# A banded-attention and expert-layer kernel: second-part loads behind a fence, wider filler matmuls, one more preparation step per piece early on, ten pieces per attention step

## The chip, the core and the metric

The kernel runs on one core of one Trainium2 chip. Its metric is the device time of one execution in microseconds (us). The core has a matrix engine (PE in the profile, with its weight loads as PEld), a vector engine (DVE), a scalar engine (ACT), a general engine (POOL) and an engine that here only issues transfers (SP). Each runs its own instructions in program order and waits on semaphores for the others.

## What is computed

```python
scores = scale * np.matmul(q, k.transpose(0, 1, 3, 2))      # 4 batches, 8 heads, 576 rows, 64 wide
scores = np.where(masks[None, :, :, :], scores, -1000000000.0)
scores = scores - np.max(scores, axis=-1, keepdims=True)
attn = np.exp(scores)
attn = attn / (np.sum(attn, axis=-1, keepdims=True) + 1e-09)
x = np.matmul(attn, v)                                      # as 2304 rows of 512
p = domain_probs / (domain_probs.sum(-1, keepdims=True) + 1e-09)
for e in range(4):
    out += p[:, e:e + 1] * (np.maximum(x @ w1[e], 0.0) @ w2[e])
```

Four heads see the last 32 positions, four see every fourth of the last 128. With the rows of the latter reordered, every head has a band 32 wide.

## The kernel before

**Attention.** The work of the band is cut into 24 steps (0 to 23), each of two groups of 192 rows. A step passes through stages that lie on different engines: `s_qk` (PE, tile sc), `s_max` (DVE: mask, maximum), `s_sub` (POOL), `s_exp` (ACT), `s_sum` (DVE: sum and reciprocal rc), `s_norm` (POOL), `s_tr` (PE transposes pt, copied by ACT to pts), `s_av` (PE, tile po, copied by ACT into the raw activations xr). The main loop runs over `n`; in each round several steps are at different stages. Steps 0 to 4 are the first part, 5 to 9 the second, 10 to 23 the third; between parts three rounds pass without a new step.

**Expert layer.** The weights come in 16 units of 256 hidden columns (`u`). A visit `(u, m)` treats one unit and one of three blocks of 768 rows. The first product (`product`, L411, tiles m1x and m1y) is done in seven block products instead of eight, on sums of the operands; the second (`mm2`, L514, tile m) adds into acc on DVE (L522). Every operand is split into a high part (ACT, L129: xh, g1h, g2h, w2h) and a low part (POOL or DVE, L126: xl, g1l, g2l, w2l). The sums of activation blocks (`x_sums`, L223) run on DVE, those of weights (`w1_sums`) on POOL. `experts` is a generator; each `yield` is a piece, about six matmuls. The first two visits are plain (no sums), 14 pieces in each of two halves; each later visit has 13 pieces: five in `mm1_b`, two in the next visit's `mm1_a`, three and three in `mm2`.

**Order.** Everything is in a fixed program order. Rounds before `START` (7) hold attention and fillers (`dummies`, L743: matmuls of the identity, 256 columns, results unused), six a round. From `START` two pieces a round are taken; after the first half `experts` pauses until round `OPEN` (15) and fillers stand in. From `OPEN` on a round takes `PACE` pieces if it begins a step, else four. After each piece `step()` does one unit of `queue`: a list of preparations (weight splits, weight sums, activation splits and sums); `later` holds those that are less urgent. When the rounds are over (gate "over"), the next visit's `begin()` closes the attention's buffers, opens more PSUM banks (gate "m1"), and puts six activation splits and two `x_sums` of the last row block into `later`. They must be done (`need(x_sums, 5)`) when visit (14, 0) hands over to (15, 0). While the buffers of the attention are in use, tile m has two PSUM banks, afterwards four.

**Loads.** SP issues nearly all transfers, in the order of the list `loads`, as `ready` allows: `load_qk` (q 192 KB, k 224 KB a step), `load_v` (two of 192 KB), `fetch_w1` and `fetch_w2` (512 KB each), probs (36 KB), masks (192 KB, from ACT's queue).

Of the kernel before, what the change touches and what calls it, by code (L numbers as in the profile page):

```python
# [18 lines left out]
GB = 6  # L19
GS = GB // 2  # L20
GW = GB * QB
PACE = 11
GAP = 3
QKB = 3
VB = 4
FILL = 6


def band_masks(S):
# [20 lines left out]
def kernel(  # L50
# [11 lines left out]
    nc = tc.nc  # L62
# [177 lines left out]
    def attention(ap, xrp, pa):  # L240
# [22 lines left out]
                ap=[row, (two.offset - one.offset, 2), col],  # L263
            )

        def load_qk(gs, k_queue):
            q_s = ap.tile([128, 2, GW], F32, tag="q", name="q_s", bufs=QKB)
            k_s = ap.tile([128, 2, GW + WINDOW], F32, tag="k", name="k_s", bufs=QKB)
            nc.sync.dma_start(out=q_s, in_=both(qT, gs, GW))
            k_queue.dma_start(out=k_s, in_=both(kT, gs, GW + WINDOW))  # L270
            for k, g in enumerate(gs):
                qk_t[g] = (q_s[:, k], k_s[:, k])
# [331 lines left out]
    def step(of=None):  # L604
        of = queue if of is None else of
        while of:
            if next(of[0][1], 0) != 0:
                return
            of.pop(0)
# [17 lines left out]
    with tc.manual_schedule():  # L627
        make_identity(nc, ident)
        nc.gpsimd.memset(eps, 1e-9)
        warm = ident.bitcast(mybir.dt.bfloat16)  # L630
# [108 lines left out]
        def dummies(n):  # L739

            for _ in range(n):
                wt = pools["m2"].tile([128, 512], F32, tag="m2", name="wt")
                nc.tensor.matmul(wt[:, :256], warm[:, :128], warm, start=True, stop=True)  # L743


        plains = [(b, [(b, p, i) for p in h0 for i in range(GP)]) for b in range(B)]
# [19 lines left out]
        qk_done = av_done = 0  # L766
        shares = []
        ready = {"w2": lambda u: u < 1 or (u - 1, 1) in w2_op}
        ready["qk"] = lambda m: m < qk_done + QKB
        ready["v"] = lambda m: m < av_done + VB and (m <= needed[1] or m <= qk_done)  # L770

        def load(what, m):
            if what == "qk":
                load_qk(steps[m], nc.sync if m else nc.scalar)
            elif what == "v":
                load_v(m, steps[m])
            elif what == "masks":
                load_masks()
            elif what == "probs":
                shares.append(load_probs())  # L780
            else:
                (fetch_w1 if what == "w1" else fetch_w2)(m)

        loads = [
# [4 lines left out]
        ]  # L789
        for m in range(needed[1] + 1, len(steps)):  # L790
            loads += [("qk", m), ("v", m)]
# [9 lines left out]
                else:  # L801
                    break

        dummies(18)
        ffn = experts(begin)
        for n in range(at(len(steps) - 1) + 5):
            load_ready()
            if START < n < OPEN:
                flush()
                holding.add(n)  # L810
                step()
            else:
                flush()
                holding.clear()
            for k, order in enumerate(stages):
                for stage, after in order:
                    m = step_at.get(n - after, -1)
                    if m >= 0 and k == (m > needed[1]):
                        stage(m, steps[m])
                        av_done += stage == order[(1, 2)[k]][0]  # L820
            if n in step_at:
                qk_done += 1
            for i, names in when.get(n, ()):
                for name in names:
                    of = first_x if i < 2 else later
                    if name is None or name == "T2":
                        prepare(x_sums, i, of=of)
                    if name is not None:
                        prepare(x_part, i, name.upper(), of=of)
            place = 0 if n <= START or n >= OPEN else len(queue)  # L830
            queue[place:place] = first_x
            first_x.clear()
            if n == 6:
                prepare(w1_split, 0)
            if n == START:
                prepare(w2_late, 0)
                prepare(w1_split, 1)
                weigh(shares[0])
            if n == START + 2:
                prepare(w2_late, 1)  # L840
            if n == OPEN:
                gate.add("open")
            if n < START:
                dummies(FILL)
                step()
                if n > 4:
                    step()
                    step()
                continue
            if "open" not in gate:  # L850
                for _ in range(2):
                    if next(ffn) == "idle":
                        dummies(3)
                step()
                continue
            for _ in range(PACE if n in step_at else 4):
                next(ffn)
                step()
                if len(queue) > 8:
                    step()  # L860
                elif later and len(queue) < 5:
                    step(later)
# [61 lines left out]
```

## Time and profile before

| | |
|---|---|
| three runs | 856.32, 856.65 (median), 857.42 us |
| the profiled execution's own time | 858.93 us |
| its span, first to last instruction | 857.1 us |
| mean granted clock of the matrix engine | 0.984 of full |

The profiled span lies 1.83 us below that execution's own time, and that execution 2.28 us above the median. The page of the profile gives busy time and instructions of each engine, then queues of transfers, then groups of instructions. Other views: busy time by stretch, instructions in order of time, waits by cause, and the chain of work that ended last. "Idle before, releaser" is the time that an engine stood still before an instruction and what ended it; "issue" means that the profile shows no event that it waited for.

### The profile page before, as it was taken

The numbers are of one execution on the slowest core, as the hardware profiler recorded it, in microseconds if no ns is written. First come the engines' busy times: TensorE is split into PE (matmuls) and PEld (weight loads), VectorE is DVE, ScalarE is ACT, GpSimd is POOL, SyncE is SP. The second block draws the span as 40 slices with busy tenths as digits, with TensorE's granted clock in tenths as the row PEclk, the third lists the DMA queues.
The fourth block names the chain that finished last, engine by engine and source line by source line (L and its number), as shares of the span: only waits on it lengthen the run. The fifth ranks groups of instructions, "written<-read, shape, count | busy, mean of one in ns | idle before, by whom it ended". The sixth has DMA issues, their size and how long they took to land.

```text
span 857.1 us, 15475 instructions
## 1 busy us (share of the span) xinstructions
PE 827.5 (97%) x6202; PEld 730.5 (85%) x6202; DVE 489.2 (57%) x1035; ACT 317.7 (37%) x753; POOL 395.4 (46%) x473
## 2 busy tenths in 40 slices
PE   8799899999999996999999999999999999999998
PEld 5678688788888885989989889899898898998986
DVE  4465556766677558655554555545555555555554
ACT  3353444554445543522323333233232242232321
POOL 4264777977676767723422431432332341342210
PEclk9699999999999998899999999999999999999999
DMA  9770343333433211310010100100100101000003
GB/s 244 210 214 22 95 135 104 89 89 93 147 89 101 80 50 50 123 50 26 25 50 25 50 25 26 50 25 25 50 25 26 49 25 50 25 26 24 1 25 123
DMA packets 46611, 59.17 MB, mean 69 GB/s; under 512 B 2873, under 2 KB 36025, under 8 KB 46539
## 3 DMA queue, kind: packets, MB, share of 16 engines
q1 hardware_dynamic: 46123, 57.75, 22.1%
q8 instruction: 49, 0.80, 0.4%
q10 hardware_dynamic: 416, 0.43, 0.1%
q14 instruction: 23, 0.19, 0.1%
HBM read 53.45 MB, written 4.72 MB: 68 GB/s over the span
## 4 chain that ended last, share of the span: by engine, by line
PE 90%; DVE 5%; POOL 1%; ACT 1%; issue 1%; DVEq 0%; POOLq 0%
PE m L514 44%; PE m1x L411 23%; PE m1y L411 17%; PE po L373 2%; PE sc L292 1%; PE wt L743 1%; PE pt L353 1%; DVE xr L223 1%; DVE acc L522 1%; DVE xl_B L126 1%; DVE hl L435 1%; ACT hh L429 0%; DVE sm L306 0%; POOL g1l L126 0%; POOL xl_T L126 0%
## 5 line engine op out<-in xcount | busy, mean ns | idle before, releaser
L522 DVE SCALAR_TENSOR_TENSOR acc<-m,pn,acc 128x512 f32<-128x512 f32 x270 | 201.9, 749 | 134.9 <-PE m L514 134.6
L514 PE MATMUL m<-w2h,hh 128*128 128x512 f32 x576 | 227.7, 395 | 4.9 <-DVE acc L522 4.5
L514 PE MATMUL m<-w2l,hh 128*128 128x512 f32 x576 | 225.7, 392 | 0.0
L126 POOL TENSOR_TENSOR g2l<-r,g2h 128x256 fp32r<-128x256 f32 x120 | 88.2, 762 | 240.1 <-PE m L514 213.0
L514 PE MATMUL m<-w2h,hl 128*128 128x512 f32 x576 | 178.6, 391 | 0.2 <-DVE hl L435 0.2
L429 ACT ACTIVATE hh<-s 128x384 fp32r<-128x384 f32 x92 | 48.3, 525 | 248.2 <-DVE s L452 190.3
L514 PEld LDWEIGHTS m<-w2h,hh 128*128 128x128 f32 x576 | 108.4, 188 | 27.8 <-DVE acc L522 7.1
L514 PEld LDWEIGHTS m<-w2h,hl 128*128 128x128 f32 x576 | 108.3, 188 | 24.3 <-DVE hl L435 0.6
L514 PEld LDWEIGHTS m<-w2l,hh 128*128 128x128 f32 x576 | 108.5, 188 | 19.5
L126 POOL TENSOR_TENSOR g1l<-r,g1h 128x256 fp32r<-128x256 f32 x93 | 70.6, 777 | 70.7 <-ACT g1h L129 70.7
L126 POOL TENSOR_TENSOR w2l<-r,w2h 128x512 fp32r<-128x512 f32 x62 | 79.7, 1302 | 47.3 <-ACT w2h L129 47.0
L471 DVE TENSOR_TENSOR s<-m1x,s 128x384 f32<-128x384 f32 x46 | 25.6, 556 | 106.8 <-PE m1x L411 101.1
L462 ACT ACTIVATE u<-m1x 128x384 f32<-128x384 f32 x46 | 22.6, 492 | 144.4 <-PE m1x L411 144.3
L435 DVE SCALAR_TENSOR_TENSOR hl<-s,hh 128x384 fp32r<-128x384 f32 x92 | 58.4, 635 | 27.6 <-ACT hh L429 27.5
L411 PE MATMUL m1x<-xh_T,g2h 128*128 128x384 f32 x152 | 51.4, 338 | 1.6 <-ACT g2h L129 1.6
L411 PE MATMUL m1x<-xh_T,g2l 128*128 128x384 f32 x152 | 51.2, 337 | 1.0 <-POOL g2l L126 1.0
L411 PE MATMUL m1x<-xl_T,g2h 128*128 128x384 f32 x152 | 51.1, 336 | 0.0
L411 PE MATMUL m1x<-xh_T,g1h 128*128 128x384 f32 x96 | 34.0, 354 | 8.8 <-DVE s L471 7.7
L411 PE MATMUL m1y<-xl_B,g2h 128*128 128x384 f32 x124 | 41.7, 336 | 0.0
L411 PE MATMUL m1y<-xh_B,g2h 128*128 128x384 f32 x124 | 41.6, 336 | 0.0
L129 ACT ACTIVATE g2h<-r 128x256 fp32r<-128x256 f32 x120 | 41.4, 405 | 0.3 <-POOL r L164 0.3
L411 PE MATMUL m1y<-xh_B,g2l 128*128 128x384 f32 x124 | 41.4, 334 | 0.0
(122 smaller groups left out, 1505.3 us busy)
## 6 DMA issues: line engine op xcount, KB each, us to landing
r<-w SPq DMA_DIRECT2D x64, 512.0 KB, 3.4
v_s<-vw SPq DMA_DIRECT2D x48, 192.0 KB, 4.6
k_s<-kT SPq DMA_DIRECT2D x23, 224.0 KB, 4.7
q_s<-qT SPq DMA_DIRECT2D x24, 192.0 KB, 4.6
out<-acc SPq DMA_DIRECT2D x18, 256.0 KB, 2.0
k_s<-kT ACTq DMA_DIRECT2D x1, 224.0 KB, 3.6
mask<-masks ACTq DMA_DIRECT2D x1, 192.0 KB, 4.2
pt__427<-probs SPq DMA_DIRECT2D x1, 36.0 KB
```

Source lines behind the costliest of these rows:

```text
L126: lo_eng.tensor_tensor(out=lo, in0=src, in1=hi.bitcast(F32), op=ALU.subtract)
L129: nc.scalar.activation(out=hi, in_=src, func=AF.Copy)
L223: nc.vector.tensor_tensor(out=quarter(i, d), in0=quarter(i, a), in1=quarter(i, b), op=ALU.subtract)
L292: nc.tensor.matmul(banks[swap][o:o + QB, i * KB:(i + 1) * KB], q_s[h, c0:c0 + QB], k_s[h, c0:c0 + KB], start=True, stop=True, skip_group_c ...
L373: nc.tensor.matmul(po[k][64 * j:64 * j + 64, o:o + QB], v_s[rows, j, 2 * i + half, :], ts_[rows, c:c + QB], start=True, stop=True,)
L411: nc.tensor.matmul(bank, w[:, k], x[:, k], start=(first and k == 0 and i == 0), stop=(last and k == 1 and i == 2), skip_group_check=True,)
L429: nc.scalar.activation(out=hi, in_=src, func=AF.Relu)
L435: nc.vector.scalar_tensor_tensor(out=lo, in0=src, scalar=0.0, in1=hi.bitcast(F32), op0=ALU.max, op1=ALU.subtract)
L462: nc.scalar.activation(out=u2, in_=x, func=AF.Copy)
L471: nc.vector.tensor_tensor(out=s5, in0=x, in1=s5, op=ALU.add)
L514: nc.tensor.matmul(po, h, w, start=(n == 0 and x == 0), stop=(n == 3))
L522: nc.vector.scalar_tensor_tensor(out=acc, in0=po, scalar=pn[:, tt, e:e + 1], in1=acc, op0=ALU.mult, op1=ALU.add,)
```

## The change

Five edits:

- `load_qk` gets a flag `fence`. For step 5 (`needed[0] + 1`) a memset of one column of the q tile is put on DVE ahead of the load, so that the load waits until DVE has come to that place, and all later entries of SP's list wait behind it. `ready["qk"]` puts this load into round 5, after the maxima of step 4.
- The list `loads` has probs ahead of the first `w2`, the second `w1` ahead of `qk` 6, and the second `w2` after `v` 7.
- Fillers have 512 columns instead of 256, and half as many: 9 for 18 at the beginning, 3 for 6 a round (4 in rounds without a new step), 2 for 3 in the pause.
- In rounds 15 and 16 a second `step()` follows each piece.
- `PACE` is 10 instead of 11.

```diff
--- before.py
+++ after.py
@@ -19,11 +19,11 @@
 GB = 6
 GS = GB // 2
 GW = GB * QB
-PACE = 11
+PACE = 10
 GAP = 3
 QKB = 3
 VB = 4
-FILL = 6
+FILL = 3
 
 
 def band_masks(S):
@@ -263,8 +263,10 @@
                 ap=[row, (two.offset - one.offset, 2), col],
             )
 
-        def load_qk(gs, k_queue):
+        def load_qk(gs, k_queue, fence):
             q_s = ap.tile([128, 2, GW], F32, tag="q", name="q_s", bufs=QKB)
+            if fence:
+                nc.vector.memset(q_s[:, 0, :1], 0.0)
             k_s = ap.tile([128, 2, GW + WINDOW], F32, tag="k", name="k_s", bufs=QKB)
             nc.sync.dma_start(out=q_s, in_=both(qT, gs, GW))
             k_queue.dma_start(out=k_s, in_=both(kT, gs, GW + WINDOW))
@@ -740,7 +742,10 @@
 
             for _ in range(n):
                 wt = pools["m2"].tile([128, 512], F32, tag="m2", name="wt")
-                nc.tensor.matmul(wt[:, :256], warm[:, :128], warm, start=True, stop=True)
+                nc.tensor.matmul(
+                    wt.rearrange("p (a b) -> p a b", a=2), warm[:, :128],
+                    warm.unsqueeze(1).to_broadcast([128, 2, 256]), start=True, stop=True,
+                )
 
 
         plains = [(b, [(b, p, i) for p in h0 for i in range(GP)]) for b in range(B)]
@@ -766,12 +771,12 @@
         qk_done = av_done = 0
         shares = []
         ready = {"w2": lambda u: u < 1 or (u - 1, 1) in w2_op}
-        ready["qk"] = lambda m: m < qk_done + QKB
+        ready["qk"] = lambda m: m < qk_done + (1 if m == needed[0] + 1 else QKB)
         ready["v"] = lambda m: m < av_done + VB and (m <= needed[1] or m <= qk_done)
 
         def load(what, m):
             if what == "qk":
-                load_qk(steps[m], nc.sync if m else nc.scalar)
+                load_qk(steps[m], nc.sync if m else nc.scalar, m == needed[0] + 1)
             elif what == "v":
                 load_v(m, steps[m])
             elif what == "masks":
@@ -783,9 +788,9 @@
 
         loads = [
             ("qk", 0), ("masks", 0), ("qk", 1), ("qk", 2), ("v", 0), ("qk", 3), ("v", 1),
-            ("qk", 4), ("v", 2), ("v", 3), ("w1", 0), ("v", 4), ("qk", 5), ("w2", 0),
-            ("probs", 0), ("qk", 6), ("w1", 1), ("v", 5), ("qk", 7), ("v", 6), ("w2", 1),
-            ("qk", 8), ("v", 7), ("qk", 9), ("v", 8), ("v", 9), ("w1", 2), ("w2", 2),
+            ("qk", 4), ("v", 2), ("v", 3), ("w1", 0), ("v", 4), ("qk", 5), ("probs", 0),
+            ("w2", 0), ("w1", 1), ("qk", 6), ("v", 5), ("qk", 7), ("v", 6), ("qk", 8),
+            ("v", 7), ("w2", 1), ("qk", 9), ("v", 8), ("v", 9), ("w1", 2), ("w2", 2),
         ]
         for m in range(needed[1] + 1, len(steps)):
             loads += [("qk", m), ("v", m)]
@@ -801,7 +806,7 @@
                 else:
                     break
 
-        dummies(18)
+        dummies(9)
         ffn = experts(begin)
         for n in range(at(len(steps) - 1) + 5):
             load_ready()
@@ -841,7 +846,7 @@
             if n == OPEN:
                 gate.add("open")
             if n < START:
-                dummies(FILL)
+                dummies(FILL if n in step_at else FILL + 1)
                 step()
                 if n > 4:
                     step()
@@ -850,12 +855,14 @@
             if "open" not in gate:
                 for _ in range(2):
                     if next(ffn) == "idle":
-                        dummies(3)
+                        dummies(2)
                 step()
                 continue
             for _ in range(PACE if n in step_at else 4):
                 next(ffn)
                 step()
+                if n <= OPEN + 1:
+                    step()
                 if len(queue) > 8:
                     step()
                 elif later and len(queue) < 5:
```

How the order of instructions moves, at three places (rows of before and of after; their line numbers differ by two).

The first is on DVE, at the end of round 4 and in round 5: sums and reciprocals of steps 3 and 4. Before:

```order
L333 TENSOR_REDUCE su<-sm 128x6
L334 TENSOR_TENSOR su<-su,eps 128x6
L337 RECIPROCAL rc<-su 128x6
L333 TENSOR_REDUCE su<-sm 128x6
L334 TENSOR_TENSOR su<-su,eps 128x6
L337 RECIPROCAL rc<-su 128x6
L126 TENSOR_TENSOR xl_B_0_583<-xr,xh_B_0_582 128x2x192
```

After:

```order
L335 TENSOR_REDUCE su<-sm 128x6
L336 TENSOR_TENSOR su<-su,eps 128x6
L339 RECIPROCAL rc<-su 128x6
L269 MEMSET q_s 128x1
L335 TENSOR_REDUCE su<-sm 128x6
L336 TENSOR_TENSOR su<-su,eps 128x6
L339 RECIPROCAL rc<-su 128x6
L126 TENSOR_TENSOR xl_B_0_532<-xr,xh_B_0_531 128x2x192
```

The memset stands behind the reciprocal of step 3 and ahead of step 4's sum; nothing else on DVE moves here.

The second is on ACT, in the rounds just after `OPEN`, around the second plain visit's results (hh<-m1x, hh<-m1y). r_1024 before and r_969 after is the same weight unit, `u` = 2. Before:

```order
L129 ACTIVATE g1h<-r_1024 128x256
L429 ACTIVATE hh<-m1x 128x384
L129 ACTIVATE g1h<-r_1024 128x256
L429 ACTIVATE hh<-m1y 128x384
L129 ACTIVATE g1h<-r_1024 128x256
L129 ACTIVATE xh_T_0_1018<-xr 128x2x192 x2
L448 ACTIVATE s_1469<-m1y 128x384
L327 ACTIVATE sm<-sm 128x384
L429 ACTIVATE hh<-s_1469 128x384
L129 ACTIVATE g2h<-r_1024 128x2x128 x4
```

After:

```order
L129 ACTIVATE g1h<-r_969 128x256 x3
L129 ACTIVATE g2h<-r_969 128x2x128 x3
L431 ACTIVATE hh<-m1x 128x384
L129 ACTIVATE g2h<-r_969 128x2x128
L129 ACTIVATE w2h<-r_971 128x512
L431 ACTIVATE hh<-m1y 128x384
L129 ACTIVATE w2h<-r_971 128x512
L129 ACTIVATE xh_T_0_963<-xr 128x2x192 x2
```

The splits g2h of the weight sums, which stood behind the next visit's hh<-s, now stand mostly ahead of the plain visit's hh<-m1x, and w2h is mixed with them.

The third is on DVE where the attention's buffers are closed: xl_B_2 are the activation splits of the last row block, xr<-xr the `x_sums`. Before:

```order
L522 SCALAR_TENSOR_TENSOR acc_828<-m_4569,pn,acc_828 128x512
L452 TENSOR_TENSOR s_4538<-m1x,s_4538 128x384
L435 SCALAR_TENSOR_TENSOR hl<-s_4538,hh 128x384
L126 TENSOR_TENSOR xl_B_2_4611<-xr,xh_B_2_4610 128x2x192
L126 TENSOR_TENSOR xl_B_2_4617<-xr,xh_B_2_4616 128x2x192
L126 TENSOR_TENSOR xl_B_2_4623<-xr,xh_B_2_4622 128x2x192
L223 TENSOR_TENSOR xr<-xr 128x2x192 x8
L522 SCALAR_TENSOR_TENSOR acc_828<-m_4636,pn,acc_828 128x512
L522 SCALAR_TENSOR_TENSOR acc_828<-m_4648,pn,acc_828 128x512
L522 SCALAR_TENSOR_TENSOR acc_828<-m_4662,pn,acc_828 128x512
```

After:

```order
L126 TENSOR_TENSOR xl_B_2_4412<-xr,xh_B_2_4411 128x2x192
L524 SCALAR_TENSOR_TENSOR acc_773<-m_4427,pn,acc_773 128x512
L524 SCALAR_TENSOR_TENSOR acc_773<-m_4441,pn,acc_773 128x512
L126 TENSOR_TENSOR xl_B_2_4438<-xr,xh_B_2_4437 128x2x192
L126 TENSOR_TENSOR xl_B_2_4463<-xr,xh_B_2_4462 128x2x192
L473 TENSOR_TENSOR s_4453<-m1x,s_4453 128x384
L223 TENSOR_TENSOR xr<-xr 128x2x192
L478 TENSOR_TENSOR u_4452<-m1y,u_4452 128x384
L437 SCALAR_TENSOR_TENSOR hl<-s_4453,hh 128x384
L437 SCALAR_TENSOR_TENSOR hl<-u_4452,hh 128x384
L223 TENSOR_TENSOR xr<-xr 128x2x192
L437 SCALAR_TENSOR_TENSOR hl<-m1x,hh 128x384
```

Three splits and eight sums in one block become one split and single or paired sums among the visit's own instructions (further sums follow, each behind an acc). The queue is filled one visit earlier, since the rounds take 14 pieces fewer.

## Rows read from the trace of the kernel before

**Rows 1.** Page: engines (busy us, share, instructions); queues (packets, MB, share).
```profile
PE 827.5 (97%) x6202; PEld 730.5 (85%) x6202; DVE 489.2 (57%) x1035; ACT 317.7 (37%) x753; POOL 395.4 (46%) x473
...
q8 instruction: 49, 0.80, 0.4%
```
**Rows 2.** Busy time by stretch: length, then PE, PEld, DVE, ACT, POOL; clock, DMA.
```profile
110.00:310.00 200.00, 196.45 (x2034) 170.62 (x2032) 131.65 (x325) 96.65 (x239) 148.07 (x172) 1.00 0.33 99
350.00:850.00 500.00, 499.94 (x2502) 452.05 (x2501) 267.17 (x421) 159.95 (x365) 165.18 (x203) 1.00 0.12 38
```
**Rows 3.** Order of time, PE, 16 to 27 us: start, length, instruction, idle before.
```profile
17.09 0.77 PE L373 MATMUL po<-pts,v_s 64*64 64x32 f32 x37 [0.57 <-issue]
...
18.18 1.03 PE L743 MATMUL wt<-ident 128*128 128x256 bf16 x6
...
19.15 0.90 PE L373 MATMUL po<-pts,v_s 64*64 64x32 f32 x48
...
26.01 0.86 PE L373 MATMUL po<-pts,v_s 64*64 64x32 f32 x24 [4.13 <-issue]
```
**Rows 4.** Transfers: packets begun in 14.25:14.50, in 23.50:23.75, and all in 17.1:23.5.
```profile
q8 instruction: 1, 0.02, 30.9%
...
q8 instruction: 1, 0.02, 26.5%
...
DMA packets 1430, 1.69 MB, mean 264 GB/s; under 512 B 101, under 2 KB 1176, under 8 KB 1429
```
**Rows 5.** Order of time, 16 to 19 us: SP's issue of step 5's q; DVE.
```profile
16.12 0.59 SPq L269 DMA_DIRECT2D q_s<-qT  x1
...
18.71 0.19 DVE L337 RECIPROCAL rc<-su 128x6 f32<-128x6 f32 x1
```
**Rows 6.** Order of time, 30 to 34.5 us, around the first product.
```profile
30.35 0.66 PE L708 MATMUL pe<-ident,pt__427 18*128 18x18 f32 x4
...
33.48 0.42 DVE L126 TENSOR_TENSOR hl<-r,hh 128x256 fp32r<-128x256 f32 x1
...
33.96 0.69 PE L411 MATMUL m1y<-xh_B,hl 128*128 128x384 f32 x1 [0.41 <-DVE hl L126]
```
**Rows 7.** Busy time by stretch, columns as in Rows 2: three stretches at a low clock.
```profile
26.01:37.57 11.56, 11.15 (x148) 9.00 (x149) 5.75 (x23) 4.97 (x14) 1.01 (x1) 0.50 0.57 138
64.91:68.28 3.37, 3.37 (x11) 3.37 (x11) 2.00 (x4) 0.00 (x0) 0.00 (x0) 0.50 0.00 0
342.39:348.63 6.24, 6.24 (x18) 5.76 (x19) 2.55 (x5) 3.81 (x9) 1.55 (x2) 0.53 0.00 1
```
**Rows 8.** Chain that ended last, in order of time: start us, us, what.
```profile
66.56 1.91 PE m1y L411 x6
68.47 1.07 PE m1x L411 x6
...
121.56 4.18 PE m L514 x18
```
**Rows 9.** Order of time, PE, 88 to 97 us.
```profile
88.78 0.45 PE L411 MATMUL m1x<-xh_T,g2h 128*128 128x384 f32 x1 [1.58 <-ACT g2h L129]
...
95.94 0.44 PE L411 MATMUL m1y<-xh_B,g1l 128*128 128x384 f32 x1 [0.81 <-POOL g1l L126]
```
**Rows 10.** Page, costliest groups: busy us, mean ns | idle before, releaser.
```profile
L129 ACT ACTIVATE g2h<-r 128x256 fp32r<-128x256 f32 x120 | 41.4, 405 | 0.3 <-POOL r L164 0.3
```
**Rows 11.** Waits in 110:310: who for whom: us in total, times, longest.
```profile
PE m L514 <- DVE acc L522: 3.2, 2, 2.1
```
**Rows 12.** Order of time, 326 to 343 us, where the attention's buffers are closed.
```profile
327.91 3.99 DVE L126 TENSOR_TENSOR xl_B<-xr,xh_B 128x384 fp32r<-128x384 f32 x3 [0.57 <-ACT xh_B L129]
...
331.82 8.08 DVE L223 TENSOR_TENSOR xr<-xr 128x384 f32<-128x384 f32 x8
...
332.53 0.44 PE L411 MATMUL m1x<-xh_T,g2l 128*128 128x384 f32 x1 [0.61 <-POOL g2l L126]
...
342.39 0.69 PE L411 MATMUL m1x<-xh_T,g1h 128*128 128x384 f32 x1 [7.65 <-DVE s L471]
```

## The prediction, made before the change was run

> **What bounds the kernel now.** I read the stretches first, then PE's instructions in order of time, then what ended PE's waits. From 350 to 850 us PE is busy for 499.94 of 500 us at the full clock, and from 110 to 310 us for 196.45 of 200 [rows 2]. So PE bounds the kernel, its useful matmuls are the same before and after, and the end moves by what PE loses ahead of 350 us: waits, and stretches in which it ran at half clock. These are few and large, so I go through them in order of time.
>
> The largest early one is 4.13 us ahead of 26.01 in the middle of step 3's `s_av`, released by nothing that the profile shows; a smaller one, 0.57 us, ends at 17.09, also inside one `s_av` [rows 3]. The operands of the first half of these 48 matmuls are those of the second, so it is not v. I take it for PE's own code. One queue moved 49 packets and 0.80 MB in all, and PE with its weight loads has 12404 instructions [rows 1]: about 253 a packet. By the list of instructions PE executes some 254 between the two waits. The packets begin at 14.25 and at 23.5, in the first 0.25 us each counts 26.5 to 30.9% of 16 engines, that is 1.1 to 1.2 us on one [rows 4], and PE goes on some 1.4 us after each end. So PE asks for a block on entering the one before it: at 17.09 for what it needs at 21.88, and the packet begins only at 23.5. In between the loads moved 1.69 MB at 264 GB/s [rows 4]: the request stood behind a backlog.
>
> The Trainium skill (DMA: Bandwidth & Descriptors, Queues, rings and completion order) says that each transfer engine takes turns between the queues that it has work for, packet by packet. By that rule a request of 17.09 would not wait 6.4 us behind another queue's loads, and the fence would shorten nothing. The rows speak against it here; what it would give is rival B.
>
> **The parts, one by one.** *The fence.* SP issued step 5's q at 16.12; now that waits for a memset behind the reciprocal of step 3, which ended at 18.90 [rows 5], and probs, `w2`, `w1` and steps 6 and 7 wait behind it on SP. The memset itself is one column on a DVE that waits between rounds: nothing. Of the 1.69 MB, step 5's q and k (416 KB), `w2` (512 KB) and probs drop out, 0.99 MB; the 0.70 MB left take 2.7 us at 264 GB/s, so the packet begins near 19.8 and PE can go on near 22.2 instead of 26.01. It reaches that place near 21.7. I take **-3.6 us**; bounds 0 (the request waits anyway) and -4.1. What is late next: `w1` of unit 1 is issued at about 21 as before; the second `w2` now comes behind steps 7 and 8, lands some 4 us after its issue and is needed near 36, so its slack is about gone, 0 to 1 us, inside the bounds. The next block of code is asked for near 22, amid the released loads, and needed near 30: just in time.
>
> *The half clock behind that wait.* From 26.01 to 37.57 PE ran at 0.50 of its clock (1.2 of 2.4 GHz), 11.56 us long [rows 7]. Six matmuls of the first product take 1.91 us there and 1.07 at the full one [rows 8]. All of it halved would be -5.6. But from the end of pe at 31.01 to that of hl at 33.90 a chain of small DVE work decides, not PE [rows 6], and po and sc are less than halved. PE at full clock will stand there for nearly 2 us instead of 0.41, and may lose the clock again. I take **-3.3**; bounds 0 and -5.6.
>
> *Fillers.* Six of 256 columns take 19.15 - 18.18 = 0.97 us [rows 3]. A 512-column matmul takes 4.18/18 = 0.23 at full clock [rows 8], so three take 0.69; if the weight load is not hidden, at most 0.97. Five rounds save 0 to 0.28 each, two rounds with four fillers lose or gain 0.3. Most of it runs into POOL's `s_norm`, which `s_tr` waits for. **-0.4**; bounds -1.4 and +0.6. In the pause four of 512 replace six of 256, more columns ahead of a wait of 1 us after which PE ran at half clock for 3.37 us [rows 7]: worth at most -1.6 if the clock stays up, I take **-0.5**, as nothing else there changes.
>
> *The further step past the gate.* In the rounds after `OPEN` PE waits 1.58 us for g2h and 0.81 for g1l [rows 9]. Both are conversions that stood too late in ACT's and POOL's order while POOL was idle before; now they come earlier (the second place in the order), and the waits go, -2.4. In exchange hh of the second plain visit stands behind three g2h of 0.405 us [rows 10], at worst +1.2, and those wait for POOL's sums. I take **-1.5**; bounds -2.4 and +1.2.
>
> *Ten pieces a step.* The same attention in 140 pieces instead of 154. Between 110 and 310 us POOL is busy for 148 of 200 us and DVE for 132 [rows 2]; a tenth more leaves both under 0.85. PE lost 3.2 us to late acc there, in two waits [rows 11]. A visit has 13 pieces, and a shift of 10 like one of 11 takes the step through nearly every place of a visit in 14 steps, so the bad ones are met again. **0**; bounds -3.2 and +4 (two more of the longest, 2.1 each).
>
> *The close of the attention.* This is the largest term. The rounds take 4 + 14 x 11 + 16 = 174 pieces before and 160 after; less 16 that belong to the plain half and the first opening, that is 12 visits and 2 pieces before, 11 visits and 1 piece after. So before, the buffers close in visit (14, 0), at whose end `x_sums` must be done, and all goes to DVE in one block: 3.99 us of splits and 8.08 of sums, during which PE waits 7.65 us (and 0.61 just ahead) [rows 12]. After it PE runs 6.24 us at 0.53 [rows 7]; 12 matmuls of the first product and six of the second cost 12 x 0.178 + 6 x 0.232 = 3.5 us at full clock [rows 8], so 2.7 are lost. Sum 10.9. After, one visit lies between, and the 12.1 us spread over its 13 pieces, 15.6 us of PE time (seven products of 1.07, six blocks of 1.39). DVE's usual load is 267/500 [rows 2], 8.3 us: together 20.4, that is 4.8 too many, of which tile m's four banks cover about four blocks, 5.6 us. So 0 to 4.8 are exposed; I take 1.4. **-9.5**; bounds -10.9 and -6.1.
>
> **Sum.** -3.6 - 3.3 - 0.4 - 0.5 - 1.5 + 0 - 9.5 = -18.8 us. The span of 857.1 becomes 838.3, the execution's own 858.93 becomes 840.1; the median of the runs, 856.65, lies 2.28 below that execution, so the forecast is **837.8 us**.
>
> **Rivals.** *B, the code wait stays or moves to the next block.* For it: the released loads come as one burst at 19 us, and the block asked for near 22 stands in it. Then -3.6 and -3.3 are lost: 844.7. Against: the backlog arithmetic above. It is also what the rule of the Trainium skill on turns (above) would give. Chance 0.14.
>
> *C, DVE cannot hold the sums even spread.* It is late by 4.8 instead of 1.4 us, and the clock falls once more (2.7): 843.9. For it: sums take 1 us while POOL works. Chance 0.13.
>
> *D, slower: too little PE work between the steps.* Place: tile m's two banks while the attention runs; acc stands on DVE behind a step's maxima and sums. Price 2.1 us a step at the longest [rows 11], over 14 steps 29.4, less the 3.2 paid already: 837.8 + 26.2 = 864.0. It decides from a mean of about 1.6 us in every step; before, 12 of the 14 cost nothing. Chance 0.04.
>
> *E, more than forecast:* the clock stays up after the pause (-1.1), no acc comes late (-3.2), the sums hide fully (-1.4): 832.1. Chance 0.07.
>
> *F, no effect:* the gate "over" falls in the same visit or the fence holds nothing back, so that only small terms remain. The order shows both moved. 856.6, chance 0.02.
>
> **How the numbers follow.** The forecast has 0.60, B 0.14, C 0.13, D 0.04, E 0.07, F 0.02. The range from 830 to 848 takes in E, and B and C with a few us more, should both hold in part. About 0.2% or 1.7 us is what a measurement here can tell from no change. Faster by more than that: 0.60 + 0.14 + 0.13 + 0.07 = 0.94; the same 0.02; slower 0.04.
>
> **What would show each step right or wrong.** PE's wait inside step 3's `s_av` is under 1 us and the code packet begins near 20; the first m1x starts near 25 instead of 30.9 with the clock at full, but for a stand near 27; g2h and g1l no longer end waits of PE after the gate; sums on DVE lie between acc rows, and no wait of PE over 3 us is left near 320 us; the steady part still has PE at 99.9%. The forecast is wrong if a wait of several us without a releaser stands elsewhere ahead of 40 us, if the clock falls near the close of the attention, or if acc ends PE's waits in many of the 14 steps.

## The result, and the profile after

The changed kernel takes 844.6 us (median of four runs, 843.5 to 845.84) against 857.03 us for the kernel before (four runs, 856.32 to 857.51): ratio 0.9856, 95% interval 0.9836 to 0.9876. That is 12.4 us less, inside the range of 830 to 848; the forecast was 18.8 us less. The profiled execution has a span of 844.1 us (857.1 before) and a time of its own of 845.84.

To see where the 13.0 us between the two profiles come from, compare the start of the same matmul of the expert layer in both; but for the fillers, PE has done the same matmuls up to it in every column. This table is worked out from PE's instructions in order of time (start in the run named minus start before, us). The other columns are experiments 5 (the change once more), 3 (no further step), 8 (also the second `w2` earlier) and 10 (ten pieces alone, in the kernel before), told below.

```
matmul (its start before)       change  again  no-step   both  pace alone
first m of the layer (40.10)     -7.50  -3.70    -7.48   -6.17     +1.37
ahead of the pause (57.15)       -3.80  -2.75    -6.28   -5.83     +1.26
behind the pause (67.96)         -5.28  -4.23    -7.70   -7.31     -0.12
107.22                           -6.59  -5.54    -9.39   -8.58     -1.84
ahead of the close (329.02)      -2.60  -4.19    -8.82   -8.06     -1.07
behind the close (354.73)       -13.04 -14.60   -20.28  -19.52    -12.55
```

Two parts of the first column are near the forecast: 7.5 us up to the first m (the terms of fence, half clock and fillers make 7.3) and 10.4 us at the close, between the last two rows (9.5). Of these gains 3.7 us were lost again between 40 and 57 us and 4.0 us between 107 and 329 us.

**The start.** Page of the change, engines and the queue of code (answers to [rows 1]); then PE in order of time, 17 to 28 us (to [rows 3]); then the code packet begun in 19.50 to 19.75 us (to [rows 4]).

```profile
PE 822.1 (97%) x6172; PEld 724.4 (86%) x6172; DVE 480.7 (57%) x1036; ACT 315.0 (37%) x753; POOL 390.4 (46%) x473
...
q8 instruction: 48, 0.79, 0.4%
```
```profile
17.30 0.43 PE L375 MATMUL po<-pts,v_s 64*64 64x32 f32 x16 [0.73 <-issue]
...
18.05 0.81 PE L745 MATMUL wt<-ident 128*128 128x512 bf16 x3
18.86 0.90 PE L375 MATMUL po<-pts,v_s 64*64 64x32 f32 x48
...
24.82 0.44 PE L413 MATMUL m1x<-xh_B,g1h 128*128 128x384 f32 x1
...
27.86 0.44 PE L413 MATMUL m1y<-xh_B,hl 128*128 128x384 f32 x1 [1.34 <-DVE hl L126]
```
```profile
q8 instruction: 1, 0.02, 31.6%
```

The 4.13 us without a releaser are gone, the packet begins four microseconds earlier than at 23.5, three wide fillers take 18.86 - 18.05 = 0.81 us, and m1x starts at 24.82 (forecast: near 25), with the stand near 27 that was forecast, 1.34 us long.

**Lost between 36 and 47 us.** The chain that ended last, in order of time, 36 to 48 us; ACT and PE in order of time there.

```profile
31.92 7.37 DMA r<-w
...
40.02 1.27 POOL w2l L126
...
42.03 0.84 POOL sm L344
...
42.92 0.71 PE pt L355 x3
```
```profile
39.31 1.15 ACT L129 ACTIVATE w2h<-r 128x512 fp32r<-128x512 f32 x2 [2.98 <-DMA r<-w]
40.37 0.47 ACT L359 ACTIVATE pts<-pt 128x384 f32<-128x384 f32 x1
...
40.89 1.06 PE L375 MATMUL po<-pts,v_s 64*64 64x32 f32 x48 [0.56 <-ACT pts L359]
...
42.92 0.71 PE L355 MATMUL pt<-ident,sm 128*128 128x128 f32 x3 [0.96 <-POOL sm L344]
```

The second `w2` is issued at 31.92 us, behind step 8's q and k and step 7's v, and lands 7.4 us later: by the trace the last load issued ahead of these (26.11 us) lands only at 34.05, and then these come first. Without the fence (experiment 1) the same load in the same place of the list took 4.75 us, and ACT waited 1.42. Here ACT stands for it, with pts and the next exponent queued behind; POOL's w2l is late with it, and s_norm behind that.

**Clock.** Busy time by stretch, columns as in rows 2, answering to [rows 2, 7]:

```profile
43.28:46.61 3.33, 3.33 (x12) 3.33 (x11) 1.03 (x2) 1.02 (x2) 2.39 (x3) 0.50 0.91 266
152.44:159.79 7.35, 7.35 (x113) 6.37 (x113) 3.74 (x18) 2.76 (x8) 4.42 (x6) 0.54 0.51 152
110.00:310.00 200.00, 195.41 (x2008) 169.52 (x2007) 122.74 (x322) 93.00 (x239) 140.16 (x169) 0.98 0.32 96
310.00:350.00 40.00, 39.47 (x200) 35.33 (x198) 34.93 (x47) 20.73 (x50) 35.43 (x37) 1.00 0.29 93
350.00:840.00 490.00, 489.94 (x2448) 442.28 (x2446) 258.89 (x410) 153.64 (x349) 154.05 (x190) 1.00 0.10 35
```

The three stretches at a low clock of before ([rows 7]) are gone; two others are there, one behind the waits for `w2`, one behind a wait for acc at 150.85. The part from 350 us on is as before.

**Past the gate, and up to the close.** POOL, ACT and PE, then DVE and PE, in order of time:

```profile
80.13 2.12 POOL L126 TENSOR_TENSOR g1l<-r,g1h 128x256 fp32r<-128x256 f32 x3
...
83.01 0.83 POOL L322 TENSOR_TENSOR sm<-sm,nm 128x384 f32<-128x384 f32 x1
...
83.87 0.52 ACT L329 ACTIVATE sm<-sm 128x384 f32<-128x384 f32 x1 [6.17 <-POOL sm L322]
84.30 0.47 ACT L450 ACTIVATE s<-m1y 128x384 f32<-128x384 f32 x1
...
85.42 0.45 PE L413 MATMUL m1x<-xh_T,g2h 128*128 128x384 f32 x1 [3.02 <-DVE s L454]
...
147.96 2.17 DVE L223 TENSOR_TENSOR xr<-xr 128x384 f32<-128x384 f32 x2
150.05 1.39 DVE L524 SCALAR_TENSOR_TENSOR acc<-m,pn,acc 128x512 f32<-128x512 f32 x2
...
150.85 0.50 PE L516 MATMUL m<-w2h,hh 128*128 128x512 f32 x1 [2.39 <-DVE acc L524]
```

The waits for g2h and g1l of [rows 9] are gone. In their place m1x waits 3.02 us, back through s on DVE and s<-m1y on ACT to an exponent that stands ahead of it on ACT, and that waits for POOL's `s_sub` (sm<-sm,nm) behind a backlog: POOL was busy with hardly a break from 66.27 us. At 150 us two activation sums stand ahead of acc on DVE, after one of 1.65 us and the last product's hl.

At the close nothing over half a microsecond is left of the 7.65 us of [rows 12]; of the sums the later ones stand one by one between acc rows:

```profile
322.24 0.74 DVE L524 SCALAR_TENSOR_TENSOR acc<-m,pn,acc 128x512 f32<-128x512 f32 x1
322.90 1.12 DVE L223 TENSOR_TENSOR xr<-xr 128x384 f32<-128x384 f32 x1
323.94 0.74 DVE L524 SCALAR_TENSOR_TENSOR acc<-m,pn,acc 128x512 f32<-128x512 f32 x1
...
327.47 0.41 PE L413 MATMUL m1x<-xh_T,g2h 128*128 128x384 f32 x1 [0.42 <-DVE s L454]
```

### The profile page after: what moved, and what is told of

Its sections match the earlier page's. It is cut to its first block, busy times and chain, and to the rows that moved or that the text cites. A ratio compares the mean times of both kernels' runs of the same rounds, so it can differ in the third digit from the quotient of the medians.

```text
span 844.1 us, 15414 instructions
## 1 busy us (share of the span) xinstructions
PE 822.1 (97%) x6172; PEld 724.4 (86%) x6172; DVE 480.7 (57%) x1036; ACT 315.0 (37%) x753; POOL 390.4 (46%) x473
## 4 chain that ended last, share of the span: by engine, by line
PE 88%; DVE 4%; DMA 2%; POOL 2%; ACT 2%; issue 1%; SPq 0%; POOLq 0%; DVEq 0%
PE m L516 44%; PE m1x L413 23%; PE m1y L413 16%; PE po L375 2%; DVE xr L223 1%; PE sc L294 1%; PE pt L355 1%; PE wt L745 1%; DMA q_s<-qT 1%; DMA r<-w 1%; DVE acc L524 1%; DMA k_s<-kT 1%; DVE hl L437 1%; POOL g1l L126 1%; ACT hh L431 0%
## 5 line engine op out<-in xcount | busy, mean ns | idle before, releaser
L437 DVE SCALAR_TENSOR_TENSOR hl<-s,hh 128x384 fp32r<-128x384 f32 x92 | 53.7, 584 | 27.3 <-ACT hh L431 27.3
L129 ACT ACTIVATE w2h<-r 128x512 fp32r<-128x512 f32 x64 | 39.1, 619 | 3.0 <-DMA r<-w 3.0
```

Of the source, the lines that this page charges most:

```text
L129: nc.scalar.activation(out=hi, in_=src, func=AF.Copy)
L437: nc.vector.scalar_tensor_tensor(out=lo, in0=src, scalar=0.0, in1=hi.bitcast(F32), op0=ALU.max, op1=ALU.subtract)
```

## The experiments

Two theories to start with. The first: the forecast's mechanisms all work, and the loss is made by the order of the second `w2` and by the further step. The rival: it is made by ten pieces a step, which crowd DVE and POOL. All times are medians; ratios are to the kernel before on the same chip, with 95% intervals.

**1. Without the fence.**
```diff
-        ready["qk"] = lambda m: m < qk_done + (1 if m == needed[0] + 1 else QKB)
+        ready["qk"] = lambda m: m < qk_done + QKB
...
-                load_qk(steps[m], nc.sync if m else nc.scalar, m == needed[0] + 1)
+                load_qk(steps[m], nc.sync if m else nc.scalar, False)
```


> The change without its fence: no memset, and step 5's q and k are loaded as early as before; list of loads, fillers, further step and ten pieces as in the change. Theory (the matrix engine's code stood behind the loads of the second part): its wait without a releaser inside step 3's s_av is back with 2.5 us or more (the change has none there), it runs at half clock behind it, and the first m1x starts at 30 to 31.5 us instead of 24.82. Since everything behind comes later, the second w2 no longer comes too late, and half of the 7.4 us is had back: 844.6 + 7.4 - 3.7 = 848.3 us, 847 to 850. Rival (the fence holds nothing back that matters; the fillers or the order of the list took the wait away): no such wait over 1 us, first m1x near 25, 844.6 us within 1.

Measured: 847.87 us, 0.9897 (0.987 to 0.9924). Code packet begun in 23.5 to 24.0 us, and the stretch up to the last transposes ahead of m1x:
```profile
q8 instruction: 1, 0.02, 14.0%
```
```profile
18.30:29.80 11.50, 11.46 (x181) 6.85 (x180) 3.33 (x9) 5.28 (x15) 2.73 (x4) 0.55 1.07 280
```
Without the fence the packet begins between 23.5 and 24.0 us again, as before the change, and m1x at 30.36. The expected wait of 2.5 us isn't there: a wait of 1.82 us for the code block ahead ended at 18.30, PE then ran at half clock, and came to the place only when the code was in. Time and start of m1x fit the theory; the form that the loss took, half clock instead of a wait, does not.

**2. The second w2 ahead of step 8.**
```diff
-            ("w2", 0), ("w1", 1), ("qk", 6), ("v", 5), ("qk", 7), ("v", 6), ("qk", 8),
-            ("v", 7), ("w2", 1), ("qk", 9), ("v", 8), ("v", 9), ("w1", 2), ("w2", 2),
+            ("w2", 0), ("w1", 1), ("qk", 6), ("v", 5), ("qk", 7), ("v", 6), ("w2", 1),
+            ("qk", 8), ("v", 7), ("qk", 9), ("v", 8), ("v", 9), ("w1", 2), ("w2", 2),
```


> The change with one entry moved in the list of loads: the second w2 ahead of step 8's q and k instead of behind its v. Theory (the 3.7 us that the lead shrinks by between 36 and 47 us come from this w2, for which ACT waits 2.98 us with the maxima's exponent and the copies of pt queued behind it): it is issued near 29.1 instead of 31.92 us, when the low part of the first w2 is done, ACT's wait for it is under 0.6 us, the matrix engine stays at the full clock from 43 to 47 us, and the time is 840.9 us, 840 to 842.5. Rival (what bounds this stretch is the bytes in flight, at 256 GB/s, not their order): step 8's k or v comes late instead and ends waits of the matrix engine before sc or po, 844.6 us within 1.

Measured: 844.98 us, 0.9857 (0.9835 to 0.9879). ACT in order of time, and two stretches:
```profile
38.56 1.14 ACT L129 ACTIVATE w2h<-r 128x512 fp32r<-128x512 f32 x2
```
```profile
27.96:34.74 6.78, 6.78 (x66) 5.90 (x66) 2.67 (x15) 0.90 (x2) 1.52 (x2) 0.52 1.09 266
43.28:46.61 3.33, 3.33 (x79) 2.97 (x71) 1.31 (x10) 2.02 (x6) 2.71 (x3) 1.00 0.47 125
```
ACT no longer waits, no wait of PE over a quarter of a microsecond is left from 28 to 50, and the clock is full at 43 to 47, so the mechanism is right. The time is not better (the rival's number, though neither k nor v ends a wait of PE there): this profile has the half clock behind the stand of 1.33 us near 28, which in the change's profile, with 1.34, cost nothing. That was the first sign that the same wait may or may not cost the clock.

**3. Without the further step.**
```diff
-                if n <= OPEN + 1:
-                    step()
```


> The change without the further preparation step in the two rounds past the gate. Theory (the further step takes the four waits of before, 1.58, 0.43, 0.81 and 1.36 us, and gives a new one of 3.0 us, since POOL has the next unit's splits and sums ahead of the attention step's subtraction, for which ACT's exponent waits with s1 behind it): the wait of 3.0 us before m1x near 85 us is gone, waits for g2h and g1l between 80 and 105 us are back with about 4 us in all: 845.7 us, 844.5 to 847. Rival (the old waits came from the later clock and order ahead of the gate and do not come back): 841.6 us, 840.5 to 843.

Measured: 841.92 us, 0.981 (0.9789 to 0.9832): better than with it, the rival's number. PE's waits between 60 and 110 us (who for whom: total, times, longest), and DVE in order of time near 146:
```profile
PE m1x L413 <- ACT g2h L129: 1.6, 1, 1.6
PE m1y L413 <- POOL g1l L126: 0.8, 1, 0.8
PE m1x L413 <- POOL g2l L126: 0.4, 1, 0.4
```
```profile
145.38 0.74 DVE L524 SCALAR_TENSOR_TENSOR acc<-m,pn,acc 128x512 f32<-128x512 f32 x1
146.04 1.68 DVE L223 TENSOR_TENSOR xr<-xr 128x384 f32<-128x384 f32 x1
```
Neither story was whole. The old waits do come back (2.8 us) and the 3.0 goes, so in its own place the step is worth next to nothing (by the table, between 67.96 and 107.22 us, 1.3 us are gained with it and 1.7 without). But every later preparation stands elsewhere too: the last two of the four activation sums now have an acc between them, acc waits between 110 and 310 us are 0.8 at the longest instead of 2.4, and the close gains 11.5 instead of 10.4.

**4. Eleven pieces a step.**
```diff
-PACE = 10
+PACE = 11
```


> The change with eleven pieces a step instead of ten. Theory (ten pieces move the closing of the attention's buffers one visit ahead and spread the twelve splits and sums; they also cost the acc wait of 2.39 us near 150 us with half a clock behind it): the sums stand in one block again, a wait of 7 to 8 us near 335 us with the clock down behind it, +10.1; the half clock near 155 us is gone and a wait of about 2 us without one stands near 160, -2.6: 852.1 us, 850.5 to 853.5. Rival (ten pieces cost nothing between 110 and 310 us, and the half clock there comes from when the waits fall, whatever the pace): 854.7 us, 853.5 to 856.

Measured: 850.86 us, 0.9933 (0.991 to 0.9956). PE in order of time at the close:
```profile
336.29 0.69 PE L413 MATMUL m1x<-xh_T,g1h 128*128 128x384 f32 x1 [7.76 <-DVE s L473]
```
The block at the close is back. An acc wait of 2.26 us stands at 156.46, so such waits don't come from the pace.

**5. The change once more.** No edit.

> The change itself, once more, to see what its clock does. Theory (the clock falls behind a wait of 1 to 3 us in one execution and not in the next, so that the same waits cost 2.5 us more or less): the waits of the matrix engine are those of the first profile (0.56 and 0.96 us before 43, 3.0 near 85, 2.4 near 151), each within 0.2 us, but at least one of the stretches at half clock (43.3 to 46.6 and 152.4 to 159.8 us) is missing or stands behind another wait; median 844 to 846.5 us, single runs 4 us apart or more. Rival (the program alone decides where the clock falls): both stretches are there again and no other, runs within 2.5 us.

Measured: 844.29 us (842.77 to 849.07, six runs), 0.9861 (0.9832 to 0.989). PE in order of time, then the stretches behind the stand before m1y (1.33 us, ended at 30.38) and behind the acc wait near 150, 2.4 us as before:
```profile
18.48 0.43 PE L375 MATMUL po<-pts,v_s 64*64 64x32 f32 x16 [1.87 <-issue]
...
151.95 0.50 PE L516 MATMUL m<-w2h,hh 128*128 128x512 f32 x1 [2.40 <-DVE acc L524]
```
```profile
30.40:36.00 5.60, 5.60 (x97) 4.74 (x98) 2.14 (x15) 0.99 (x3) 1.53 (x2) 0.70 0.40 92
152.00:160.00 8.00, 8.00 (x126) 6.45 (x127) 5.36 (x21) 3.60 (x10) 7.27 (x9) 1.00 0.66 203
```
The theory holds for the clock: the waits of PE of 3.0 and 2.4 us are the same, but the clock stays full behind the acc wait. It falls behind a code wait that took 1.87 us instead of 0.73 (0.62 from 20.04 to 24.59), and behind the stand before m1y, at which it had stayed full in the change. These made the expert layer later. ACT still waited 2.22 us for the second `w2`, but the two waits of PE behind it (0.56 and 0.96 us), which were expected again, did not arise. From 107 to 329 us the same work took 223.15 us here and 225.80 in the change's profile: that half clock cost 2.65 us. Its runs have mean clocks from 0.997 (842.77 us) to 0.986 (849.07 us).

**6. Fillers of before.** 18, six and three of 256 columns (the change's diff of `dummies` undone).
```diff
-FILL = 3
+FILL = 6
...
-                nc.tensor.matmul(
-                    wt.rearrange("p (a b) -> p a b", a=2), warm[:, :128],
-                    warm.unsqueeze(1).to_broadcast([128, 2, 256]), start=True, stop=True,
-                )
+                nc.tensor.matmul(wt[:, :256], warm[:, :128], warm, start=True, stop=True)
...
-        dummies(9)
+        dummies(18)
...
-                dummies(FILL if n in step_at else FILL + 1)
+                dummies(FILL)
...
-                        dummies(2)
+                        dummies(3)
```

> The change with the fillers of before: 18, six a round and three in the pause, of 256 columns. Theory (the wide fillers are worth their few tenths a round; in the pause they keep the clock up): six take 0.97 us where three take 0.75 and four 0.96; the first m1x starts 0.3 to 0.8 later, at 25.1 to 25.6; from the end of the pause on the matrix engine is at half clock for some 3 us again: 846.3 us, 845 to 848. Rival (fillers have no part in it): first m1x within 0.2 of 24.82, full clock at 61 to 64 us, 844.6 within 1. A third way: the eighteen more matmuls move the places where a block of code is asked for, and a wait without a releaser of 1 us or more stands in a place where the change has none: 847 to 849.

Measured: 848.06 us, 0.9889 (0.9869 to 0.9908). PE in order of time, step 3's `s_av`, at the very matmul of the 4.13 us of [rows 3]:
```profile
22.96 0.55 PE L375 MATMUL po<-pts,v_s 64*64 64x32 f32 x24 [1.01 <-issue]
```
The same matmul in experiment 10, with the same fillers and no fence:
```profile
26.50 0.61 PE L373 MATMUL po<-pts,v_s 64*64 64x32 f32 x24 [3.88 <-issue]
```
This is the fence at the old place: 4.13 and 3.88 us without it, 1.01 with it. The time and this wait are the third way of the expectation. The next block is now late too (0.83 us in step 5's `s_qk`), and the clock fell between 30 and 40 us and after 150. The pause disproves a part of the theory: with the old fillers the clock stays full behind it.

**7. Forty narrow fillers at the start of the kernel before.**
```diff
+        for _ in range(40):
+            wt = pools["m2"].tile([128, 512], F32, tag="m2", name="wt")
+            nc.tensor.matmul(wt[:, :32], warm[:, :128], warm[:, :32], start=True, stop=True)
```


> The kernel before with 40 more fillers of 32 columns at the very beginning, where the matrix engine waits for the first loads. Theory (its waits without a releaser are for its own code, in blocks of some 254 instructions): both waits stand 40 matmuls earlier in the order, the small one inside s_qk instead of s_av (near its 19th of 48), the large one near the 41st of the 48 of s_av of the step ahead (step 2), in a place that had no wait; the large one still ends near 25 us, since the same loads are ahead of the packet; 855 to 860 us. Rival (the large wait is for v or for another operand of step 3's s_av): it stays at the 24th matmul of step 3's s_av.

Measured: 863.86 us (one run). PE in order of time:
```profile
20.70 0.41 PE L292 MATMUL sc<-k_s,q_s 64*32 64x64 f32 x20
23.23 0.45 PE L292 MATMUL sc<-k_s,q_s 64*32 64x64 f32 x28 [2.12 <-issue]
...
27.03 1.38 PE L373 MATMUL po<-pts,v_s 64*64 64x32 f32 x41
29.81 0.43 PE L373 MATMUL po<-pts,v_s 64*64 64x32 f32 x7 [1.40 <-issue]
```
Both waits moved back by 39 or 40 matmuls, to behind the 20th of an `s_qk` and the 41st of an `s_av` that had none. They belong to the count of instructions, so to PE's code. The time was misjudged: the fillers ran into the first step and everything began some 6 us later.

**8. Second w2 ahead, and no further step** (edits 2 and 3), and the same again as a run of its own.

> The change with the second w2 ahead of step 8's q and k, and without the further preparation step. Theory (the two faults of the change are independent: waits of 1.9 us between 36 and 43 us go with the first, the 3.0 us near 85 with the second, and each wait that goes is one occasion less for the clock to fall): no wait over 0.6 us between 28 and 60, none over 1.7 between 60 and 110, 839.5 us, 837 to 841.5. Rival (the lead won ahead of 60 us is given back, since the attention then waits for its loads): the waits reappear before sc or po and the time is 842 us, 841 to 843.5.

> The second w2 ahead and no further step, once more on the chip on which the late normalizing runs: 839.4 us, 838 to 841, with the same waits, and code waits and half clock where they fall this time.

Measured: 839.36 us, 0.9785 (0.9763 to 0.9807), and 838.3 us, 0.9789 (0.9766 to 0.9811): the best, faster than both kernels. Alone, edit 3 gave 0.981 and edit 2 0.9857 against the change's 0.9856, so without the further step edit 2 looks worth 2 us, and with it nothing; the intervals don't tell these apart. The waits for `w2` are gone and so is the 3.0 near 85 us, as expected; the stand of 1.34 us before m1y and the 1.05 us behind the pause, which the expectation left out, are still there.

**9. Probs normalized a round later**, on top of 8.
```diff
                 prepare(w1_split, 1)
+            if n == START + 1:
                 weigh(shares[0])
```

> The second w2 ahead and no further step, and the normalizing of probs (four transposes and five small DVE instructions, about 2 us of DVE ahead of the low parts that the first product waits for) one round later. Theory (the stand of 1.33 us before m1y near 28 us is made by these five, and the clock falls behind stands): the stand is under 0.4 us, the first m of the expert layer starts 1 us earlier, 838.2 us, 836.5 to 839.5. Rival (DVE's small instructions now stand between the maxima of the next step, and that chain gets later): a wait of about 1 us before pt or sc instead, 839.4 within 1.

Measured: 839.99 us, 0.9799 (0.978 to 0.9818): no gain. PE in order of time:
```profile
28.25 0.44 PE L413 MATMUL m1y<-xh_B,hh 128*128 128x384 f32 x1 [0.52 <-ACT hh L129]
...
29.35 0.44 PE L413 MATMUL m1y<-xh_B,hl 128*128 128x384 f32 x1 [0.67 <-DVE hl L126]
```
The one stand became two, of 1.2 us together, plus a code wait of 0.9 us: the first ends with ACT's split, the second with DVE's low part of it. The time is the rival's, but its wait before pt or sc is not there.

**10. Ten pieces a step alone, in the kernel before.**
```diff
-PACE = 11
+PACE = 10
```

> The kernel before with ten pieces a step and nothing else. Theory (the close of the attention is worth about 10 us by itself, and the acc wait with its half clock near 150 us comes with the further step, not with the pace): the wait of 7.65 us before m1x near 342 us is gone, waits for acc between 110 and 310 us are 3 us in all or less, 847.5 us, 846 to 849.5. Rival (ten pieces crowd DVE between 110 and 310 us whatever else is done): waits for acc of 5 us or more there, 850 to 853.

Measured: 844.75 us, 0.9849 (0.9827 to 0.9871): by itself as much as the whole change, and below the 846 to 849.5 expected. PE's waits between 110 and 350 us:
```profile
PE m L514 <- DVE acc L522: 2.0, 3, 0.8
PE sc L292 <- ACT xr L389: 1.4, 2, 1.1
PE m1x L411 <- DVE s L471: 0.5, 1, 0.5
```
The 7.65 us at the close are gone and so are the acc waits of 1.36, 2.1 and 1.07 us of before; none over 0.8 took their place. The rival falls. By the table 11.5 of the 12.55 us behind the close come from the close itself; at the pause, which the pace does not touch, 1.4 us come from a clock that stayed full this time.

## Why the prediction was right, and where it was off

*The close of the attention, -9.5:* right, and the largest term. 10.4 us in the change, 11.5 in the pace-alone kernel; the sums hide better than assumed (0.5 us exposed, not 1.4). A slip in its working hardly matters: seven products of 1.07 and six blocks of 1.39 are 15.8 us, not 15.6.

*The fence, -3.6, and the half clock behind it, -3.3:* the mechanism is shown by experiments 1, 6, 7 and 10. The size varies: the packet begins between 19.5 and 22.0 us in the nine profiles with the fence (23.6 to 24.0 in the kernel before and experiments 1 and 10, without it), and the small wait ahead of it, 0.57 us before, took 0.36 to 1.87 in nine profiles with wide fillers, at one and the same matmul. Up to the first m the kernel gains 7.5 us in the change's profile and 3.7 in experiment 5, of 7.3 forecast; over the seven profiles with fence and wide fillers whose order up to there is nearly the same (all but experiment 9) it is 3.0 to 7.5. So the 7.5 next to the forecast of 7.3 is partly luck, and rival B came true in part: some of the wait moved to the neighbouring blocks. That the median, 844.6, is B's number, 844.7, is chance, for the wait that B expects in step 3 or the next block is not there in the change's profile. The rule on turns of the Trainium skill (DMA: Bandwidth & Descriptors, Queues, rings and completion order) does not explain these runs: by it the fence would shorten nothing, and with the fillers of before 3.88 us became 1.01.

The Trainium skill (Runtime: NRT & Kernel Launch, Instruction fetch mechanics) says that code comes in blocks of 256 instructions, the next one fetched while the current one runs, and that this is mostly hidden. The size agrees with the waits, which stand 127 matmuls with their weight loads apart, and in experiment 7, within one, at the same count of matmuls as before; hidden it is not here, while the loads fill the transfer engines.

*"Its slack is about gone, 0 to 1 us":* this is the first step that failed. The second `w2` was 2.98 us late for ACT, and with the half clock behind it the lead shrank by 3.7 us in the change's profile (by 1.2 in experiment 3, which has the same order and kept the clock). The forecast took the landing time of before, 4 us; with more loads still on their way ahead of it, it was 7.4 (5.3 in experiment 5).

*Fillers, -0.4, and the pause, -0.5:* experiment 6 puts the wide fillers at 3.8 us between medians, more than both terms. In its profile the first m starts 0.8 us later than in experiment 5, and from 107 to 329 us, with half clock behind the acc wait, it takes 2.9 us more; how much of the 3.8 is the fillers and how much the clock's chance stays open. The gain of 1.5 us behind the pause is no effect of the fillers: 1.4 us of it are there with the old fillers too, in experiments 6 and 10.

*The further step, -1.5:* the second step that failed. It costs 2.7 us between the medians of experiment 3 and the change (3.9 by the ratios). Against experiment 5, whose clock is full in these stretches, 0.8 us of it is seen between 107 and 329 us, where the acc waits are 3.2 us in all against 2.0, and 1.0 at the close. The forecast looked at the two rounds in which it stands; the gain there is also 1.7 us in the pace-alone kernel, which has no further step (its acc wait at 107.22 us went with the pace). What it left out is that an extra step moves every later preparation, among them the activation sums that now stand ahead of acc near 150 us.

*Ten pieces a step, 0 (-3.2 to +4):* right within its bounds. Alone it loses 0.8 us between 107 and 329 us. Of the 4.0 us lost there in the change, 2.65 are the half clock behind the acc wait, which experiment 5 does not have; it loses 1.35, the kernels without the further step 0.6 (experiment 3) and 0.5 us (8).

Taken together, the change's profile has -7.5 up to the first m, +3.7 to the pause, -1.5 there, -1.3 past the gate, +4.0 up to the close and -10.4 at it. The time fell inside the range because the largest term held; what the forecast is off lies in the two losses: the second `w2`, and up to the close a half clock by chance, the further step and 0.8 us of the pace. Experiment 8, the forecast's edits without the two faults, measures 838.3 and 839.4 us, against the 837.8 forecast for all of them. The pace alone makes 12.6 of these 18 to 19 us; fence, order of loads and fillers make about 6.

## What to carry to other kernels

Cost a moved preparation by where everything behind it in the same queue will stand, round by round, not by the wait it is meant to remove; and measure each edit alone, for here one line by itself gave as much as the whole change, and another took a fifth to a third of that back. When loads are held back, re-time the last load of the held group with all the held bytes ahead of it. A wait of the matrix engine without a releaser that moves with the count of instructions was its own code here, and holding loads back ahead of it shortened it.

## What the runs showed of the hardware

The clock's answer to a wait is not fixed by the program. Behind the same acc wait of 2.4 us near 150 us, PE ran at 0.54 of its clock for 7.35 us in one execution of the change and at the full clock in the next (experiment 5); behind the stand of 1.3 us before m1y it was the other way round, full in the first and 0.70 from 30.40 to 36.00 us in the next. A prediction can give the clock's share only as a chance times a price. By estimate the price here is 1.7 to 3.4 us a time (3.33 us at 0.50 and 7.35 at 0.54, each times what is missing of the clock); the one pair that shows it directly gives 2.65. And the wait for one code block varies by over a microsecond between executions of one program, 0.73 and 1.87 us at the same matmul. Such a stretch can start behind it, as in experiment 5, but need not: behind 1.87 us in experiment 8 the clock was 1.00 from 18.12 to 24.00 us.
